# An attention and two-layer kernel: the gate's products are put in another order and alternate between two banks

## The chip, the cores and the metric

The kernel runs on one core of a Trainium2 chip. Its time is the device time of one execution in microseconds (us), taken over several executions. Five engines work beside each other, each through its own instructions in order: TensorE (PE; its weight loads are shown as PEld), VectorE (DVE), ScalarE (ACT), GpSimd (POOL) and SyncE (SP, which issues the DMAs). They wait for each other by semaphores. TensorE writes its results into PSUM, which has 8 banks of 512 float32 values in each of 128 partitions; VectorE and ScalarE read them from there.

## The reference

```
def _moe_ref(x, w1, w2, w3, w_out):
    a = x @ w1
    b = x @ w2
    h = a * b @ w3
    return (h @ w_out).astype(np.float32)

def _moe2_ref(x, w_in, w_out, g_ln):
    h = x @ w_in
    # solu = h * softmax(h), then a layer norm over the row with the gain g_ln
    ...
    return (ln @ w_out).astype(np.float32)

def reference(...):
    attn_out = _attn_ref(...)        # banded attention: a window of 128 keys and 4 sink keys
    x = ...                          # 4 batches of 768 tokens, 512 columns
    x = _moe_ref(x=x, ...)           # 512 -> 1024 -> 1024 -> 512
    return _moe2_ref(x=x, ...)       # 512 -> 1024 -> 512
```

The stage of this case is the gate: `a = x @ w1`, `b = x @ w2` and their product element by element, for 3072 tokens, 512 columns in and 1024 out.

## The kernel before, in words

The kernel has four parts behind each other: attention (which also multiplies `w3` and `moe_w_out` together), the gate, the hidden layer, and the second network with its norm. Each engine's instructions behind the attention come from one list of tasks. A planner (`arrange`, line 49) puts them in order. It gives each task a duration and a due time (its rank) and lets each engine take the task with the lowest rank among those that are ready by its own reckoning. In that reckoning a bank is free once its readers are done, bank by bank. The waits themselves are set when the program is built, and go by the tile that an instruction touches.

Every large matrix product is done in 7 products of half matrices instead of 8 (line 41, `FACTORS`). A factor is a half of the matrix or a sum of halves, and each is split into a high and a low part, so that three matmuls together give float32 accuracy. These splits are line 365 on VectorE (low part) and line 158 on ScalarE (high part); the sums are line 368.

In the gate a batch has four groups of columns, m = 0 to 3. A group has 14 products: k = 1 to 7 for both weights, z = 0 for `w1` and z = 1 for `w2`. In this text (k,z) is such a product. A product is 6 matmuls of 128x128 weights over 384 columns into one bank. Products go one on the other: on bank Y first 1, then 6, 7 and 4 are added to what is there; on bank Z first 5, then 3; on bank X stands 2 alone. What has to be kept from a state in between is copied out by ScalarE (line 158, `copy`) or added to something by VectorE (line 948, `two`) before the next product goes on top. So every product on Y but the first of a group waits for a reader of the product before it.

The 8 banks are four tiles of two banks each (line 888). Tile 0 holds X and Y of z = 0 (X0, Y0), tile 1 holds Z0 and X1, tile 2 holds Y1 and Z1; tile 3 is unused in the gate before the change. The batches come in the order 2, 3, 0, 1 (line 988). Beside the products VectorE, ScalarE and GpSimd convert and split the gate's remaining weights (in the first batch), convert later weights (in the second and third) and split the next batch's tokens.

`both` (line 984) is the order in which products are put on the list; it also sets (`when`) when each factor's parts are due. `product` (line 974) picks the bank, lines 1067 to 1096 the copies and additions of a group.

Of the kernel before, what the change touches and what calls it, by code (L numbers as in the profile page):

```python
# [123 lines left out]
def attention_moe_kernel(  # L124
# [27 lines left out]
    PE, DVE, ACT, POOL, SP = nc.tensor, nc.vector, nc.scalar, nc.gpsimd, nc.sync  # L152
# [9 lines left out]
    def ns_of(eng, n):  # L162

        return {"ACT": 188 + .834 * n, "DVE": 140 + 1.055 * n, "POOL": 159 + 2.2 * n}[eng]
# [12 lines left out]
    def path(stack, banded):  # L177
# [5 lines left out]
        xop = hold.rearrange("p (s u c n) -> p s u c n", s=7, u=2, c=2)  # L183

        xlie = {n: i for i, n in enumerate((1, 6, 5, 4, 0, 3, 2))}
# [224 lines left out]
        def pair_factors(side, pair, seven):  # L410

            four = pair.rearrange("p a (b n) -> p (a b) n", b=2)
            return factors(
                side, [four[:, i] for i in range(4)], lambda n: (seven[:, n, 0], seven[:, n, 1]), (four, seven)
            )
# [54 lines left out]
        def x_factors(b):  # L470
            x = x_t[b]
            blk = [x[:, 2 * k:2 * k + 2, S // 2 * n:S // 2 * (n + 1)] for n in range(2) for k in range(2)]
            return factors("right", blk, lambda n: (xop[:, xlie[n], 0], xop[:, xlie[n], 1]))
# [390 lines left out]
        else:  # L864
            general_fold()
            general_attention()
            for n in range(4):
                w, m = ("w1", "w2")[n % 2], n // 2
# [21 lines left out]
        bank = [t[:, i] for t in four_banks for i in range(2)]  # L890
# [34 lines left out]
        def op(eng, ns, rank, outs, ins, f, *args, after=0, both=False, then=None):  # L925

            r = set().union(*(toks(a) for a in ins)) if ins else set()
            w = set().union(*(toks(a) for a in outs))
            if then is not None:
                r.add(then)  # L930
            tasks.append((eng + "+" * (eng == "POOL" or both), ns, rank, "stage", f, args, r - w, w, after))

        def dma(rank, out, in_, then=None):

            size = 4
            for d in out.shape:
                size *= d
            op("SP", max(475, size / 320), rank, [out], [in_], lambda: SP.dma_start(out=out, in_=in_), after=2300, then=then)

        def copy(rank, out, in_, cols, eng="ACT"):  # L940
            if eng == "ACT":
                op("ACT", ns_of("ACT", cols), rank, [out], [in_], acopy, out, in_)
            else:
                op("DVE", ns_of("DVE", cols), rank, [out], [in_], lambda: DVE.tensor_copy(out=out, in_=in_))

        def two(eng, rank, out, a, b, cols, o=ALU.add):
            op(
                eng, ns_of(eng, cols), rank, [out], [a, b], lambda: engines[eng].tensor_tensor(out=out, in0=a, in1=b, op=o),  # L948
                both=eng == "DVE" and not {a.tensor.name, b.tensor.name} & banks,
            )  # L950
# [20 lines left out]
        X, Y, Z = 0, 1, 2  # L971
        BANK = {1: Y, 6: Y, 7: Y, 4: Y, 2: X, 5: Z, 3: Z}

        def product(k, z, rank, ns, width, left, right):

            b = bank[3 * z + BANK[k]][:, 0:width]
            (lh, ll), (rh, rl) = left, right
            items = []
            for c in range(len(lh)):
                items += [(lh[c], rh[c]), (lh[c], rl[c]), (ll[c], rh[c])]  # L980
            op("PE", ns, rank, [b], [*lh, *ll, *rh, *rl], run, b, items, k in (1, 2, 5))
            return b

        both = [(1, 0), (1, 1), (2, 0), (6, 0), (2, 1), (6, 1), (5, 0), (7, 0), (5, 1), (7, 1), (4, 0), (3, 0), (4, 1), (3, 1)]
        when = {}
        for i, (k, z) in enumerate(both):
            when.setdefault(k, i)
# [1 line left out]
        TH = S // 2  # L989
        now = 0.0  # L990
# [37 lines left out]
        for bi, b in enumerate(order):  # L1028
            if bi >= 2:
                dma(now - 40000, slots[b % 2], xd[b].rearrange("p c n -> p (c n)"))  # L1030
            if bi:
                parts_of(x_factors(b), 768, part_rank(1, now, MM), sums="DVE")
            for m in range(4):
                if bi == 0 and m > 1:
                    for u, w in enumerate(("w1", "w2")):
                        for i in range(2):
                            convert((w, m + 4 * i), pairs[np_ % 3][:, i], u, now - 18000 + 1000 * u)
                        parts_of(pair_factors("left", pairs[np_ % 3], group(w, groups[m])), 0, part_rank(0, now, MM))
                        np_ += 1
                if bi in (1, 2):  # L1040
                    for _ in range(2):
                        key = later.pop(0)
                        d = pairs[0][:, key[1] % 2]
                        rank = now + 20000
                        convert(key, d, 0, rank)
                        if key[0] == "wout":
                            sc = g_sb[:, key[1]:key[1] + 1]
                            op("ACT", 600, rank, [d], [g_sb], acopy, d, d, sc)
                        dma(rank, (win_d if key[0] == "win" else wout_d)[key[1]], d)
                if bi == 3 and m == 2:  # L1050
                    for k in range(4):
                        piece = wpiece[k % 3].rearrange("p (m h n) -> p m h n", m=2, h=2)
                        for h in range(2):
                            dma(now - 8000, piece[:, :, h, :], wf_d[k + 4 * h].rearrange("p (m n) -> p m n", m=2))
                        four = piece.rearrange("p m h n -> p (m h) n")
                        seven = wfop[k]
                        parts_of(
                            factors("left", [four[:, i] for i in range(4)], lambda n: (seven[:, n, 0], seven[:, n, 1]), (four, seven)),
                            0, lambda n, kind, k=k: now + 8000 + 2000 * k, sums="DVE",
                        )  # L1060
                gw = [group(w, groups[m]).rearrange("p s u (c n) -> p s u c n", c=2) for w in ("w1", "w2")]
                p_, u2, u3, cc = tmp[0:2], tmp[2:4], tmp[4:6], tmp[6]

                def send(i, t, rank):
                    dma(rank, ab_d[b][i][m], t)

                for k, z in both:
                    l, r = FACTORS[k]
                    bk = product(
                        k, z, now, MM, TH, [[gw[z][:, l, u, c, :] for c in range(2)] for u in range(2)],  # L1070
                        [[xop[:, xlie[r], u, c, :] for c in range(2)] for u in range(2)],
                    )
                    now += MM
                    if k in (1, 6, 7):
                        copy(now, {1: p_, 6: u2, 7: u3}[k][z], bk, TH)
                    if k == 2:
                        two("DVE", now + 2000, p_[z], bk, p_[z], TH)
                        if z:
                            two("DVE", now + 5000, p_[0], p_[0], p_[1], TH, ALU.mult)
                            send(0, p_[0], now + 5000)  # L1080
                    if k == 7:
                        two("DVE", now, u3[z], bank[3 * z + Z][:, 0:TH], u3[z], TH)
                        if z:
                            two("DVE", now + 5000, u3[0], u3[0], u3[1], TH, ALU.mult)
                            send(3, u3[0], now + 5000)
                    if k == 4:
                        if z:
                            two("DVE", now + 1000, cc, cc, bk, TH, ALU.mult)
                            send(1, cc, now + 5000)
                        else:  # L1090
                            copy(now + 1000, cc, bk, TH)
                    if k == 3:
                        two("DVE", now + 1000, u2[z], bk, u2[z], TH)
                        if z:
                            two("DVE", now + 5000, u2[0], u2[0], u2[1], TH, ALU.mult)
                            send(2, u2[0], now + 5000)
# [48 lines left out]
        for g in range(7 * B):  # L1145
            bi, i = divmod(g, 7)
            b, k = order[bi], seq[i]
# [10 lines left out]
            for z in range(2):  # L1158
                p_, u2, u3, cc = tmp[4 * z:4 * z + 4]
                bk = product(  # L1160
                    k, z, now, MM, TH, [[wfop[c][:, l, u, z * P:(z + 1) * P] for c in range(4)] for u in range(2)],
                    [[t[:, u, c] for c in range(4)] for u in range(2)],
                )
# [101 lines left out]
        for c in range(2 * PAIRS):  # L1265
# [6 lines left out]
            if c in (7, 11, 15, 19):  # L1272
                k = (c - 7) // 4
# [145 lines left out]
```

## Time and profile before

| | us |
|---|---|
| median of 3 runs | 927.65 (926.5 to 927.68) |
| the profiled execution | 927.59 |
| its span in the profile | 925.2 |
| TensorE busy | 888.6 (96%) |
| VectorE busy | 700.0 (76%) |
| ScalarE busy | 548.8 (59%) |
| GpSimd busy | 183.4 (20%) |
| the gate's first matmul, the hidden layer's last | 263.4, 638.1 |

All places in the trace are in us from the start of the span. A row of a stretch shows its bounds and length, then the busy us (and number of instructions) of PE, PEld, DVE, ACT and POOL, the granted clock of TensorE as a share of full speed, the busy share of the DMA engines, and GB/s. A row in order of time shows start, length, engine, line, operation, output and inputs with shape, how many instructions are drawn together, and in brackets how long the engine stood idle before, and what ended that. A row of waits shows who waited for whom, the us in total, how often, and the longest. Buffer numbers are left out there, so that all banks are called bank.

### The profile page before, as it was taken

To read this page: it belongs to the slowest core of one execution; us is meant where nothing else is said; L and a number is where in the kernel's file an instruction comes from. 1 tells how busy PE (TensorE), PEld (TensorE's weight loads), DVE (VectorE), ACT (ScalarE), POOL (GpSimd) and SP (SyncE) were. 2 spreads that over 40 slices of the span, in tenths; PEclk is the share of its full clock that TensorE was granted. 3 is DMA by queue.
4 is the path that set the end of the run, shared out by engine and by line. 5 is a ranking of instruction groups with operands and counts; after the bars stand their busy time and mean duration, and the time that the engine had idled before them with its cause. 6 is when DMAs were issued, how large, how long until landed. Compare 5 with 4: busy or idle time off the path is not lost.

```text
span 925.2 us, 15584 instructions
## 1 busy us (share of the span) xinstructions
PE 888.6 (96%) x5392; PEld 749.8 (81%) x5392; DVE 700.0 (76%) x1646; ACT 548.8 (59%) x1251; POOL 183.4 (20%) x243
## 2 busy tenths in 40 slices
PE   7999999999999899999998999999999999999996
PEld 3555665665579898989888999999888888999996
DVE  6988888676958786773776897794788877898761
ACT  6887877765746444752543566563667576755441
POOL 2664655451225322120000000000010011000000
PEclk9999999999999999999999999999999999999999
DMA  7566657632236367563132265443243343454411
GB/s 273 182 232 235 204 188 252 215 123 80 69 100 184 128 203 240 191 214 125 56 130 76 85 208 188 158 146 124 104 146 127 125 160 137 172 194 143 177 58 61
DMA packets 84760, 143.72 MB, mean 155 GB/s; under 512 B 6976, under 2 KB 58432, under 8 KB 82240
## 3 DMA queue, kind: packets, MB, share of 16 engines
q1 hardware_dynamic: 84672, 142.64, 46.1%
q8 instruction: 44, 0.72, 0.3%
q14 instruction: 44, 0.36, 0.1%
HBM read 95.43 MB, written 47.19 MB: 154 GB/s over the span
## 4 chain that ended last, share of the span: by engine, by line
PE 82%; DVE 12%; DMA 2%; issue 2%; ACT 1%; POOL 1%; SPq 0%; DVEq 0%; ACTq 0%; POOLq 0%
PE bank L155 56%; PE s L155 11%; PE pa L155 6%; PE pat L644 4%; DVE arF L948 3%; PE bank L1233 2%; DVE hold L365 2%; DVE g L365 2%; PE pn L656 1%; PE pn L650 1%; DVE ar L368 1%; DVE sa L600 1%; DMA arF<-in_moe_w_in_dram 1%; DVE ring L661 1%; DMA qk<-in_qk_dram 1%
## 5 line engine op out<-in xcount | busy, mean ns | idle before, releaser
L155 PE MATMUL bank<-hold,g 128*128 128x384 f32 x2016 | 360.7, 338 | 15.4 <-DVE arF L948 11.1
L155 PEld LDWEIGHTS bank<-hold,g 128*128 128x128 f32 x2016 | 349.8, 189 | 26.4 <-DVE arF L948 19.2
L155 PE MATMUL bank<-g,hold 128*128 128x512 f32 (+1 forms) x1080 | 202.2, 342 | 0.6 <-ACT ar L158 0.5
L155 PEld LDWEIGHTS bank<-g,hold 128*128 128x128 f32 x1080 | 169.2, 190 | 22.3 <-ACT ar L158 1.0
L158 ACT ACTIVATE arF<-bank 128x384 f32<-128x384 f32 (+1 forms) x160 | 80.8, 519 | 115.5 <-PE bank L155 80.5
L615 ACT ACTIVATE sa<-sa,st 128x288 f32<-128x288 f32 (+1 forms) x192 | 95.7, 501 | 20.3 <-DVE st L600 17.4
L600 DVE CUSTOM_DVE_ANT_0 sa<-s,masks 128x288 f32<-128x288 f32 (+1 forms) x192 | 76.8, 418 | 23.9 <-PE s L155 23.6
L948 DVE TENSOR_TENSOR arF<-bank,arF 128x384 f32<-128x384 f32 x96 | 53.0, 554 | 51.7 <-PE bank L155 23.4
L365 DVE TENSOR_TENSOR hold<-ar,hold 128x384 fp32r<-128x384 f32 (+2 forms) x137 | 84.6, 648 | 8.5 <-ACT hold L158 8.2
L1221 POOL TENSOR_TENSOR stt<-stt,half 128x1 f32<-128x1 f32 x24 | 17.3, 721 | 371.0 <-DVE stt L1219 363.2
L158 ACT ACTIVATE hold<-ar 128x384 fp32r<-128x384 f32 (+2 forms) x137 | 75.4, 586 | 18.0 <-DVE ar L368 13.8
L155 PE MATMUL s<-qk 64*128 64x288 f32 (+2 forms) x384 | 75.0, 439 | 8.0 <-DMA qk<-in_qk_dram 6.0
L158 ACT ACTIVATE ar<-bank 128x256 f32<-128x256 f32 (+1 forms) x80 | 33.8, 423 | 73.9 <-PE bank L155 73.5
L155 PE MATMUL bank<-g,g 128*128 128x256 f32 x504 | 66.3, 285 | 3.9 <-DVE ar L948 2.2
L661 DVE COPY ring<-pat 128x512 f32<-128x512 f32 (+1 forms) x96 | 60.9, 640 | 11.3 <-PE pat L644 10.9
L155 PEld LDWEIGHTS bank<-g,g 128*128 128x128 f32 x504 | 62.5, 192 | 5.5 <-DVE ar L948 3.0
L155 PEld LDWEIGHTS s<-qk 64*128 64x128 f32 x384 | 34.0, 193 | 35.9 <-issue 15.0
L155 PE MATMUL s<-hold 128*128 128x512 f32 x192 | 59.5, 423 | 0.0
L155 PE MATMUL pa<-ring,vn 128*64 128x256 f32 (+1 forms) x448 | 56.1, 357 | 1.5 <-DVE ring L661 1.0
L644 PE MATMUL pat<-identr,sa 128*128 128x128 f32 x352 | 56.5, 281 | 0.0
L948 DVE TENSOR_TENSOR ar<-bank,ar 128x256 f32<-128x256 f32 (+1 forms) x60 | 28.4, 475 | 32.9 <-ACT ar L158 19.1
L368 DVE TENSOR_TENSOR ar<-ar 128x256 f32<-128x256 f32 (+3 forms) x92 | 51.5, 571 | 0.8
(97 smaller groups left out, 1150.4 us busy)
## 6 DMA issues: line engine op xcount, KB each, us to landing
qk<-in_qk_dram SPq DMA_DIRECT2D x15, 1088.0 KB, 5.1
raw<-in_moe_w_dram SPq DMA_DIRECT2D x24, 512.0 KB, 5.1
abd<-arF SPq DMA_DIRECT2D x64, 192.0 KB, 2.0
lnd<-arF SPq DMA_DIRECT2D x48, 256.0 KB, 2.2
ar<-lnd SPq DMA_DIRECT2D x8, 1024.0 KB, 5.6
vn<-in_v_dram SPq DMA_DIRECT2D x16, 384.0 KB, 3.2
arF<-abd SPq DMA_DIRECT2D x8, 768.0 KB, 5.0
ar<-abd SPq DMA_DIRECT2D x8, 768.0 KB, 4.7
```

The lines of the kernel that those rows point to most:

```text
L155: PE.matmul(o, lhsT=l, rhs=r, start=start, stop=stop, skip_group_check=True)
L158: ACT.activation(out=o, in_=i, func=AF.Copy, scale=s)
L365: eng.tensor_tensor(out=lo, in0=src, in1=fl(hi), op=ALU.subtract)
L368: eng.tensor_tensor(out=out, in0=a, in1=b, op=ALU.add if sign > 0 else ALU.subtract)
L600: DVE.tensor_tensor_reduce(out=sa[s][:, h, :n], in0=s_bank[s_at(s, h)][:, :n], in1=m_qb[j, h], op0=ALU.add, op1=ALU.min, scale=-scale, sca ...
L615: ACT.activation(out=a[:, h, :n], in_=a[:, h, :n], func=AF.Exp, scale=-1.0, bias=st_t[s][:, h:h + 1], accum_out=rs_t[p, j // 2][:, i:i + 1],)
L644: PE.transpose(pt[:, h, u, :], a[:, h, o:o + P], ident)
L650: PE.transpose(pn[0:n + 2 * SINKS, s % 2, :], a[:, 256 - n:256 + 2 * SINKS], ident)
L661: DVE.tensor_copy(out=ring[:, :, 2 * j + u0:2 * j + 2, :], in_=pat_t.pop(s)[:, :, u0:, :])
L948: eng, ns_of(eng, cols), rank, [out], [a, b], lambda: engines[eng].tensor_tensor(out=out, in0=a, in1=b, op=o),
L1221: op("POOL", 550, rank + 900, [st[7]], [st[6]], lambda: POOL.tensor_tensor(out=st[7], in0=st[6], in1=half, op=ALU.pow))
L1233: PE.transpose(bk[:, i * P:(i + 1) * P], e[:, (4 * g + i) * P:(4 * g + i + 1) * P], ident)
```

## The change

Four things change, all in the gate. The order of the products of a group becomes 1, 2, 6, 5, 7, 3, 4, each for z = 0 and then z = 1. In groups with odd m, what went to bank Y goes to bank 6 + z, the two banks of tile 3. What is kept of product 5 is copied out by ScalarE behind 5, and the addition behind 7 reads Y and not Z; before, 7 was copied and Z was read. And the order of the factors' due times follows, since `when` is made from `both`.

```
-        def product(k, z, rank, ns, width, left, right):
+        def product(k, z, rank, ns, width, left, right, other=False):
-            b = bank[3 * z + BANK[k]][:, 0:width]
+            b = bank[6 + z if other and BANK[k] == Y else 3 * z + BANK[k]][:, 0:width]
...
-        both = [(1, 0), (1, 1), (2, 0), (6, 0), (2, 1), (6, 1), (5, 0), (7, 0), (5, 1), (7, 1), (4, 0), (3, 0), (4, 1), (3, 1)]
+        both = [(k, z) for k in (1, 2, 6, 5, 7, 3, 4) for z in range(2)]
...
-                        [[xop[:, xlie[r], u, c, :] for c in range(2)] for u in range(2)],
+                        [[xop[:, xlie[r], u, c, :] for c in range(2)] for u in range(2)], m % 2 == 1,
...
-                    if k in (1, 6, 7):
-                        copy(now, {1: p_, 6: u2, 7: u3}[k][z], bk, TH)
+                    if k in (1, 6, 5):
+                        copy(now, {1: p_, 6: u2, 5: u3}[k][z], bk, TH)
...
-                        two("DVE", now, u3[z], bank[3 * z + Z][:, 0:TH], u3[z], TH)
+                        two("DVE", now, u3[z], bk, u3[z], TH)
```

On TensorE, an inner group of the last batch stands in the program before like this, from (1,1) to (5,0). bank0, bank1, bank2 and bank3 are the four tiles; x5 or x6 are the matmuls of a product, x11 five of one and six of the next.

```order
L155 MATMUL bank2_3011<-hold_74,g23_3003 128x384 [waits DVE_49]
L155 MATMUL bank2_3011<-hold_74,g23_3003 128x384 x5
L155 MATMUL bank0_3009<-hold_74,g23_3003 128x384 [waits Activation_49]
L155 MATMUL bank0_3009<-hold_74,g23_3003 128x384 x11
L155 MATMUL bank1_3010<-hold_74,g23_3003 128x384 x6
L155 MATMUL bank2_3011<-hold_74,g23_3003 128x384 [waits Activation_49]
L155 MATMUL bank2_3011<-hold_74,g23_3003 128x384 x5
L155 MATMUL bank1_3010<-hold_74,g23_3003 128x384 [waits DVE_49]
L155 MATMUL bank1_3010<-hold_74,g23_3003 128x384 x5
```

The products are (1,1), (2,0) with (6,0), (2,1), (6,1) and (5,0). The first and the last wait for VectorE; (2,1) and (5,0) are both on bank1, with (6,1) between.

An odd group of the last batch now, from (1,0) and (1,1) to (5,1):

```order
L155 MATMUL bank3_3012<-hold_74,g01_73 128x384 x12
L155 MATMUL bank0_3009<-hold_74,g01_73 128x384 [waits Activation_49]
L155 MATMUL bank0_3009<-hold_74,g01_73 128x384 x5
L155 MATMUL bank1_3010<-hold_74,g01_73 128x384 x6
L155 MATMUL bank3_3012<-hold_74,g01_73 128x384 [waits Activation_49]
L155 MATMUL bank3_3012<-hold_74,g01_73 128x384 x11
L155 MATMUL bank1_3010<-hold_74,g01_73 128x384 [waits DVE_49]
L155 MATMUL bank1_3010<-hold_74,g01_73 128x384 x5
L155 MATMUL bank2_3011<-hold_74,g01_73 128x384 x6
```

The wait of (1,1) is gone, and between (2,1) and (5,0) on bank1 stand both 6 on bank3.

The second half of an even group of the last batch now, from (7,0) to (4,1):

```order
L155 MATMUL bank0_3009<-hold_74,g23_3003 128x384 x6
L155 MATMUL bank2_3011<-hold_74,g23_3003 128x384 [waits Activation_49]
L155 MATMUL bank2_3011<-hold_74,g23_3003 128x384 x5
L155 MATMUL bank1_3010<-hold_74,g23_3003 128x384 x6
L155 MATMUL bank2_3011<-hold_74,g23_3003 128x384 [waits DVE_49]
L155 MATMUL bank2_3011<-hold_74,g23_3003 128x384 x5
L155 MATMUL bank0_3009<-hold_74,g23_3003 128x384 x6
L155 MATMUL bank2_3011<-hold_74,g23_3003 128x384 [waits DVE_49]
L155 MATMUL bank2_3011<-hold_74,g23_3003 128x384 x5
```

(7,1), (3,1) and (4,1) are all on bank2 (Y1, Z1, Y1), with one product between each two, and each waits for a reader of the one before.

On VectorE, the rows before between the additions of X0 and of X1 in an even group of the last batch (line 365 are splits):

```order
L948 TENSOR_TENSOR arF_3004<-bank0_3009,arF_3004 128x384 [waits PE_49,Activation_49]
L365 TENSOR_TENSOR g23_3003<-arF_3004,g23_3003 128x512 [waits DMAHW5_49,Activation_49]
L365 TENSOR_TENSOR g01_73<-ar1_75,g01_73 128x2x256 [waits Activation_49] x2
L948 TENSOR_TENSOR arF_3004<-bank1_3010,arF_3004 128x384 [waits PE_49]
L948 TENSOR_TENSOR arF_3004<-arF_3004 128x384 [waits DVE_49]
```

The same place of the same group now, with the split that stands ahead of the first addition:

```order
L365 TENSOR_TENSOR g01_73<-ar1_75,g01_73 128x2x256 [waits Activation_49]
L948 TENSOR_TENSOR arF_3004<-bank0_3009,arF_3004 128x384 [waits PE_49]
L365 TENSOR_TENSOR g01_73<-ar1_75,g01_73 128x2x256 [waits Activation_49]
L948 TENSOR_TENSOR arF_3004<-bank1_3010,arF_3004 128x384 [waits PE_49]
L365 TENSOR_TENSOR g01_73<-ar1_75,g01_73 128x2x256 [waits Activation_49]
L948 TENSOR_TENSOR arF_3004<-arF_3004 128x384 [waits DVE_49]
```

One split stands between the two additions where three stood.

## Rows read from the trace of the kernel before

**Rows 1.** The page's first part, TensorE: busy us, share of the span, instructions.

```profile
PE 888.6 (96%) x5392; PEld 749.8 (81%) x5392; DVE 700.0 (76%) x1646; ACT 548.8 (59%) x1251; POOL 183.4 (20%) x243
```

**Rows 2.** Stretches: the gate's four batches in order, then the hidden layer.

```profile
263.40:329.60 66.20, 62.69 (x337) 59.63 (x338) 51.11 (x85) 35.91 (x70) 25.56 (x25) 0.97 0.48 150
329.60:393.20 63.60, 60.65 (x337) 57.81 (x336) 45.79 (x85) 37.26 (x75) 15.06 (x12) 1.00 0.67 224
393.20:456.20 63.00, 60.02 (x338) 58.10 (x337) 36.73 (x70) 26.23 (x54) 5.36 (x4) 1.00 0.40 134
456.20:521.70 65.50, 60.42 (x338) 57.95 (x338) 47.19 (x96) 29.61 (x61) 0.00 (x0) 1.00 0.32 101
521.70:640.00 118.30, 118.30 (x680) 117.75 (x679) 97.98 (x200) 66.71 (x141) 0.00 (x0) 1.00 0.52 166
```

**Rows 3.** Who waited for whom in the gate, TensorE's matmuls.

```profile
PE bank L155 <- DVE arF L948: 11.1, 16, 1.2
PE bank L155 <- ACT arF L158: 2.6, 4, 0.9
```

**Rows 4.** Order of time, TensorE, the last batch.

```profile
455.68 1.73 PE L155 MATMUL bank<-hold,g 128*128 128x384 f32 x9
458.02 5.50 PE L155 MATMUL bank<-hold,g 128*128 128x384 f32 x30 [0.61 <-DVE arF L948]
464.02 9.63 PE L155 MATMUL bank<-hold,g 128*128 128x384 f32 x54 [0.51 <-DVE arF L948]
474.40 5.48 PE L155 MATMUL bank<-hold,g 128*128 128x384 f32 x30 [0.74 <-DVE arF L948]
480.78 9.64 PE L155 MATMUL bank<-hold,g 128*128 128x384 f32 x54 [0.91 <-DVE arF L948]
491.16 5.48 PE L155 MATMUL bank<-hold,g 128*128 128x384 f32 x30 [0.74 <-DVE arF L948]
497.55 9.66 PE L155 MATMUL bank<-hold,g 128*128 128x384 f32 x54 [0.91 <-DVE arF L948]
507.88 14.30 PE L155 MATMUL bank<-hold,g 128*128 128x384 f32 x80 [0.67 <-DVE arF L948]
```

**Rows 5.** Order of time, TensorE, the third batch.

```profile
392.71 1.73 PE L155 MATMUL bank<-hold,g 128*128 128x384 f32 x9
395.04 5.49 PE L155 MATMUL bank<-hold,g 128*128 128x384 f32 x30 [0.61 <-DVE arF L948]
401.50 45.27 PE L155 MATMUL bank<-hold,g 128*128 128x384 f32 x252 [0.97 <-DVE arF L948]
447.75 8.44 PE L155 MATMUL bank<-hold,g 128*128 128x384 f32 x47 [0.98 <-DVE arF L948]
```

**Rows 6.** Order of time, VectorE, ahead of TensorE's pause at 497.55.

```profile
495.14 0.68 DVE L365 TENSOR_TENSOR g<-arF,g 128x512 fp32r<-128x512 f32 x1
495.74 1.29 DVE L365 TENSOR_TENSOR g<-ar,g 128x512 fp32r<-128x512 f32 x2
496.94 0.55 DVE L948 TENSOR_TENSOR arF<-bank,arF 128x384 f32<-128x384 f32 x1
```

**Rows 7.** Order of time, VectorE, a quiet group of the third batch.

```profile
425.19 0.56 DVE L948 TENSOR_TENSOR arF<-arF,bank 128x384 f32<-128x384 f32 x1 [1.59 <-PE bank L155]
425.66 0.55 DVE L948 TENSOR_TENSOR arF<-bank,arF 128x384 f32<-128x384 f32 x1
426.25 0.56 DVE L948 TENSOR_TENSOR arF<-arF 128x384 f32<-128x384 f32 x1
...
430.83 0.56 DVE L948 TENSOR_TENSOR arF<-bank,arF 128x384 f32<-128x384 f32 x1 [0.48 <-PE bank L155]
```

**Rows 8.** Order of time, TensorE, two pauses of the first batch.

```profile
302.93 11.87 PE L155 MATMUL bank<-hold,g 128*128 128x384 f32 x66 [0.92 <-ACT arF L158]
...
322.04 2.89 PE L155 MATMUL bank<-hold,g 128*128 128x384 f32 x12 [0.58 <-ACT arF L158]
```

**Rows 9.** Order of time, VectorE, an addition of two SBUF operands in the first batch.

```profile
271.84 1.51 DVE L948 TENSOR_TENSOR arF<-arF 128x384 f32<-128x384 f32 x1
```

## The prediction, made before the change was run

> **What bounds the kernel now.** I read the page's first part, then a table of stretches, then the waits, then the order of time on single engines.
>
> The page gives TensorE 96% of the span [rows 1]. A change that only moves waits can therefore win little, and only where TensorE pauses. The stretches show where that is [rows 2]. After the gate, the hidden layer runs 680 matmuls in 118.30 us with TensorE busy all the time: 0.174 us from one start to the next. The gate runs from 263.4 to 521.7, which is 258.3 us for 224 products of 6 matmuls, 1344 in all. At 0.174 these need 233.9, so 24.4 us are lost there. By batch of 336 matmuls (58.5 us) the loss is 7.7, 5.1, 4.5 and 7.0 us in the order of the four rows.
>
> The waits of that stretch say who ends the pauses [rows 3]: mostly VectorE's line 948 (the additions that read a bank), then ScalarE's line 158 (the copies).
>
> In the order of time on TensorE the counts name the product that pauses [rows 4, 5]. In the last batch stretches of 30 and 54 matmuls alternate, 5 and 9 products. Five products are (1,1), (2,0), (6,0), (2,1), (6,1); nine run from (5,0) to the next group's (1,0), where (k,z) is product k of weight z. So TensorE stops at two places per group: ahead of (1,1), which I call pause A, and ahead of (5,0), pause B. Each is sized by start + count x 0.174 against the next start. For the last batch: 0.77, 0.78, 0.98, 1.16, 0.98, 1.17 and 0.93, together 6.8 of the 7.0 lost. For the third batch: 0.76, 1.24, and 2.40 over the 252 matmuls to 447.75, together 4.4 of 4.5.
>
> Pause B is not a wait for the bank of (5,0) itself. That bank, Z0, shares a tile with X1, and the program's wait falls on the addition that reads X1, the result of (2,1), one product earlier. In the row order that addition stands behind three splits. The trace has them from 495.14, one of 0.68 and two in 1.29; the addition starts at 496.94, and TensorE resumes at 497.55, 0.06 after it ends [rows 4, 6]. In the quiet third batch the same wait costs nothing: 401.50 to 447.75 is one row, and VectorE stood idle 0.48 us before the addition at 430.83 [rows 5, 7]. Pause A is two additions behind each other (425.19 and 425.66) that are both held until (3,1) has ended, since Y1 and Z1 share a tile. It costs about 0.4 even with an idle VectorE: 2.40 less one pause B of 1.2 leaves 1.2 for three of them [rows 5, 7].
>
> **The change part by part.** No instruction is added or removed: matmuls, copies and additions keep their number and size. The copy of 7 becomes a copy of 5, and the addition that read Z reads Y. That costs nothing, since both are the same form.
>
> *Odd groups (m = 1, 3).* Y lies in the fourth tile, with nothing else in it. All waits there reach back two products or more. (1,1) has no wait of its own, and (5,0) waits for X1 with two products between instead of one, that is 1.04 us more. Pauses A and B go.
>
> *Even groups (m = 0, 2).* (1,1) now waits for (3,1) of the odd group before, with three products between, and (5,0) for X1 with two. Pauses A and B go here as well. But 3 ahead of 4 and 2,2,6,6 put new close waits on shared tiles, with one product between: (6,0) on the addition of X0, (3,1) on that of Y1, (4,1) on that of Z1. Counting them in the row order over all eight even groups gives 20, 11 of them in the last two batches. The trace of before bounds such a wait at 0 (the quiet B) and 1.17 (B behind three splits). One addition fits with about 0.07 us to spare (pause A's 0.4 less the 0.47 between its two additions). For (3,1) and (4,1) the additions of 7 and 3 stand one behind the other with at most a split between, so I take the value near the quiet row, 0.1; for (6,0) one split of 0.68 [rows 6] can stand ahead, so I take 0.5. In the last two batches that is 8 x 0.1 + 3 x 0.5 = 2.3.
>
> ScalarE gets more waits with one product between too, (5,1) and (7,1) on copies. Before, (2,0) has this wait on the copy of (1,0) in most groups, and none of the rows of the last two batches stops there [rows 4, 5]. I take 0; behind one split of ScalarE it could be 0.4 each.
>
> *Last two batches:* 11.2 of pauses go, 2.3 come: 8.9 gained.
>
> *First two batches:* 12.8 are lost. The granted clock of 0.97 over 66.2 us is 2.0 of that and stays [rows 2]; it is 1.00 elsewhere in the gate. The remaining 10.8 are mixed. Of TensorE's 11.1 us of idle behind VectorE's additions [rows 3], the pauses listed for the last two batches hold 7.65 (0.61, 0.97, 0.98; 0.61, 0.51, 0.74, 0.91, 0.74, 0.91, 0.67); 3.45 is left for the first two. Scaled by pause per idle (11.2 / 7.65) that is about 5 us of pauses of kinds A and B. ScalarE's 2.6 of idle lies here, with pauses like those at 302.93 and 322.04 [rows 8]; about 3.8 us by the same scale. Products of two groups are shuffled there because the weights' factors come late, and afterwards they still are. I let the 5 go, 1.5 of ScalarE's go, and charge the 9 other close waits 0.3 each (more splits stand about there): 5 + 1.5 - 2.7 = 3.8. Bounds: 0 to 9.
>
> In this stretch VectorE is slower as well: an addition of two SBUF operands took 1.51 us at 271.84 and 0.56 at 426.25 [rows 7, 9], and POOL is busy 25.56 us in the first batch and not at all in the last [rows 2]. *GPSIMD Engine Reference* of the Trainium skill, section 1 Specifications, says that GpSimd's SBUF interfaces are shared with VectorE and contend with its instructions that have two SBUF inputs; the trace agrees (1.51 against 0.56). By that rule a close wait in the first batch stays dear in any order, and without that batch's part (about 1.5) the time would be 916.4.
>
> *What cover there is.* Nothing behind the gate absorbs the gain: the hidden layer's TensorE row is full, and the order behind the gate is that of before. Its VectorE is busy 97.98 of 118.30 [rows 2], so there is room to follow an earlier start. In the gate VectorE's 47.19 us would stand in about 60 in the last batch, 79%.
>
> *Sum:* 8.9 + 3.8 = 12.7. The profiled execution took 927.59 us (span 925.2 and 2.4 around it): 927.6 - 12.7 = 914.9. The median of the runs is 927.65, so the same.
>
> **The rivals.**
> 1. *The close waits cost what B costs now.* B cost 0.78, 1.16, 1.17, 1.24 and about 1.2 in five of the last eight groups and nothing in three: 0.69 on average. 20 x 0.69 = 13.8 against 11.2 + 6.5 = 17.7: 3.9 gained, 923.7. This is also the case in which the change doesn't do what it says: three products lie between any two on a bank, yet in even groups only one between two on a tile. For it: VectorE is busy 77% of the first batch and 72% of the second and the last [rows 2]. Against it: the splits stand in the first half of a group, the new waits mostly in the second.
> 2. *All goes but the clock.* If no close wait were felt, 24.4 - 2.0 = 22.4 would go: 905.2. Against it: a split of 0.68 and only 0.07 to spare. The Trainium skill's page *PSUM — Partial Sum Buffer*, section *PSUM bank collisions raise a hardware error*, has software guard PSUM by bank and quadrant. By that rule alone there would be no close wait here, and this rival would be the forecast; the trace differs, since pause B ends with an addition on another bank.
> 3. *Slower: the pairs in the fourth tile.* In odd groups the products of a pair, say (1,0) and (1,1), write one tile, so the reader of the first is held until the second has ended, 1.04 us at the head of ScalarE's or VectorE's queue. Four pairs in eight groups are 33 us of held queues, with the splits for the next factors behind them. It decides from the point where more than 17.7 of the 33 reaches TensorE. At three quarters it is 25: 7 slower, 934.6. Against it: ScalarE is idle about half of the gate and the reuse of a pair's banks is two products off.
>
> **How the numbers follow.** Forecast 0.65 (its own range 909 to 920), rival 1 0.19, rival 2 0.11, rival 3 0.05. Low 905.0 takes in rival 2, high 923.5 half of rival 1. A difference of 0.2%, 1.9 us, is what a measurement of this kernel can tell. Faster: forecast, rival 2 and most of rival 1, 0.92. Same: a part of rival 1, 0.03. Slower: rival 3, 0.05.
>
> **What the profile after would show.** On TensorE the alternating stretches of 30 and 54 are gone and odd groups run through. What pauses are left stand in even groups ahead of (6,0), (3,1) or (4,1), and in the first batch. The idle behind line 948 falls from 11.1 to about 4, the gate to about 246 us, and the hidden layer keeps 118.3. If pauses of near 1 us stand at (3,1) and (4,1), rival 1 holds. If odd groups stop as well, or ScalarE's copies hold TensorE, rival 3 does. If TensorE stops behind the gate, the cover was wrong.

## The result, and the profile after

The changed kernel takes 911.2 us (median of 4 runs, 909.7 to 912.79), the kernel before, in runs on the same chip, 927.08 (924.66 to 927.68). The ratio is 0.983, 95% interval 0.981 to 0.986. The forecast was 914.9, with a range of 905.0 to 923.5.

The profiled execution of the changed kernel took 910.68, with a span of 908.9. The page's first part, as [rows 1]:

```profile
PE 881.7 (97%) x5392; PEld 748.2 (82%) x5392; DVE 697.8 (77%) x1646; ACT 546.3 (60%) x1251; POOL 183.1 (20%) x243
```

All instruction counts are those of before. The span is 16.3 us shorter, TensorE's busy time only 6.9; the rest of it was idle time of TensorE. The four batches of the gate and the hidden layer, as [rows 2]:

```profile
262.08:324.56 62.48, 60.12 (x336) 58.14 (x337) 46.53 (x80) 35.26 (x71) 24.90 (x24) 1.00 0.48 154
324.56:385.38 60.82, 59.90 (x337) 58.08 (x337) 47.66 (x88) 34.98 (x68) 14.42 (x11) 1.00 0.67 221
385.38:445.18 59.80, 59.25 (x337) 58.20 (x337) 37.21 (x73) 27.81 (x56) 6.50 (x5) 1.00 0.48 160
445.18:504.96 59.78, 59.22 (x338) 58.20 (x337) 47.06 (x98) 28.99 (x62) 0.00 (x0) 1.00 0.34 111
504.96:623.26 118.30, 118.30 (x680) 117.75 (x680) 97.90 (x200) 66.71 (x142) 0.00 (x0) 1.00 0.51 166
```

The gate takes 242.9 us where it took 258.3. By batch the gain is 3.7, 2.8, 3.2 and 5.7 us, and 4.0, 2.4, 1.3 and 1.3 of loss against the pure 58.5 are left. The hidden layer has kept its 118.30. So 15.4 of the 16.3 us come from the gate; its start is 1.3 us earlier and the time behind it 0.4 longer. Who waited for whom in the gate, TensorE's matmuls, as [rows 3]:

```profile
PE bank L155 <- DVE arF L948: 3.2, 5, 1.2
...
PE bank L155 <- ACT arF L158: 0.9, 2, 0.5
```

The idle behind VectorE's additions fell from 11.1 us in 16 pauses to 3.2 in 5. In order of time on TensorE, from the gate's start to the hidden layer, as [rows 4, 5]:

```profile
262.08 32.16 PE L155 MATMUL bank<-hold,g 128*128 128x384 f32 x180 [0.91 <-DVE ar L703]
294.67 3.40 PE L155 MATMUL bank<-hold,g 128*128 128x384 f32 x18 [0.43 <-ACT arF L158]
299.26 9.88 PE L155 MATMUL bank<-hold,g 128*128 128x384 f32 x54 [1.19 <-DVE arF L948]
309.87 26.88 PE L155 MATMUL bank<-hold,g 128*128 128x384 f32 x150 [0.74 <-DVE arF L948]
337.01 30.03 PE L155 MATMUL bank<-hold,g 128*128 128x384 f32 x168 [0.26 <-DVE arF L948]
367.59 27.36 PE L155 MATMUL bank<-hold,g 128*128 128x384 f32 x156 [0.55 <-DVE arF L948]
395.43 54.09 PE L155 MATMUL bank<-hold,g 128*128 128x384 f32 x306 [0.47 <-ACT arF L158]
449.99 171.82 PE L155 MATMUL bank<-hold,g 128*128 128x384 f32 x984 [0.47 <-DVE arF L948]
```

The alternation of 30 and 54 matmuls is gone. In the last two batches only two pauses are long enough for a row of their own: at 395.43 ahead of (7,1) of the third batch's first group, and at 449.99 ahead of (6,0) of the last batch's first group, both even. VectorE ahead of the second:

```profile
447.51 0.56 DVE L948 TENSOR_TENSOR arF<-arF 128x384 f32<-128x384 f32 x1
447.98 1.49 DVE L365 TENSOR_TENSOR hold<-ar,hold 128x384 fp32r<-128x384 f32 x3
449.38 0.55 DVE L948 TENSOR_TENSOR arF<-bank,arF 128x384 f32<-128x384 f32 x1
```

This is the picture of [rows 6] again: three splits ahead of the addition, and TensorE resumes 0.06 us after it. The reader of X0, one product behind, now has the place that the reader of X1 had.

### The profile page after: what moved, and what is told of

The parts are those of the page before. It is cut to its first block, busy times and chain, and to the rows that moved or that the text cites. A ratio compares the mean times of both kernels' runs of the same rounds, so it can differ in the third digit from the quotient of the medians.

```text
span 908.9 us, 15588 instructions
## 1 busy us (share of the span) xinstructions
PE 881.7 (97%) x5392; PEld 748.2 (82%) x5392; DVE 697.8 (77%) x1646; ACT 546.3 (60%) x1251; POOL 183.1 (20%) x243
## 4 chain that ended last, share of the span: by engine, by line
PE 84%; DVE 10%; ACT 2%; DMA 2%; issue 1%; SPq 0%; POOL 0%; DVEq 0%; ACTq 0%
PE bank L155 62%; PE s L155 10%; PE pa L155 5%; PE pat L644 3%; PE bank L1233 2%; DVE hold L365 2%; DVE sa L600 1%; DVE arF L948 1%; PE pn L656 1%; DVE ring L661 1%; PE pn L650 1%; DVE ar L368 1%; DMA raw<-in_moe_w_dram 1%; DVE g L365 1%; DMA qk<-in_qk_dram 1%
## 5 line engine op out<-in xcount | busy, mean ns | idle before, releaser
L155 PE MATMUL bank<-hold,g 128*128 128x384 f32 x2016 | 355.3, 336 | 5.3 <-DVE arF L948 3.2
L158 ACT ACTIVATE hold<-arF 128x384 fp32r<-128x384 f32 (+2 forms) x82 | 41.9, 553 | 18.1 <-DVE arF L368 5.7
```

The lines of the kernel that those rows point to most:

```text
L155: PE.matmul(o, lhsT=l, rhs=r, start=start, stop=stop, skip_group_check=True)
L158: ACT.activation(out=o, in_=i, func=AF.Copy, scale=s)
```

## The experiments

All eight are compared with the kernel before on the same chip: 926.6 us in the first four, 926.56 in the last four. The theory was that the waits go by the tile of two banks: a reader (a copy or an addition) starts when the last product put on its tile before it has ended, and the next product on that tile waits for the reader. By the theory TensorE pauses where only one other product stands between these two products; such a wait is called a close wait. The rivals were that the gain comes from the alternation itself (the bank), and that VectorE's queue holds the product in any arrangement.

**Order alone.** The new order and copies, Y always in its own bank.

```
-                        ... for u in range(2)], m % 2 == 1,
+                        ... for u in range(2)], False,
...
```

> The new order of products alone; bank Y is not alternated. Theory (tile): a pause is a wait for a reader of the same two-bank tile with one product between, priced by what stands ahead of that reader. By the row order the waits of that kind on VectorE are 26 here (23 before the change, 20 after), those on ScalarE 44 (18, 24). Pauses A and B go by the order, the close waits of even groups then stand in all groups: about 915 (913 to 919), gate about 247 us. Rival (bank): what counts is that two products on one bank have three others between, so without the second bank pause A returns in all groups and the time is 920 to 924.

Measured: 911.15 us (910.45 to 912.45), ratio 0.984 [0.982, 0.985]. TensorE in order of time, from late in the second batch to the gate's end:

```profile
364.67 44.10 PE L155 MATMUL bank<-hold,g 128*128 128x384 f32 x246 [1.19 <-ACT arF L158]
410.06 3.40 PE L155 MATMUL bank<-hold,g 128*128 128x384 f32 x18 [1.30 <-DVE arF L948]
413.63 94.61 PE L155 MATMUL bank<-hold,g 128*128 128x384 f32 x538 [0.17 <-ACT arF L158]
```

The 538 matmuls from 413.63 to 508 need 93.6 at 0.174 and took 94.6. As a whole program, the new order without alternation brings all that the change brings (911.15 against 911.2; the profiled gates take 244.0 and 242.9). Both the theory's number (my size of a close wait) and the bank rival were too high. Counted in the row order, this kernel has 26 close waits for VectorE, the changed kernel 20 and the kernel before 23, so their number alone is not what costs.

This is not the changed kernel with one thing taken away. Without the second bank the planner puts (2,0) ahead of (1,0) in nearly every group, so two products and not one stand between (6,0) and the last one before it on its tile, and no pause stands ahead of (6,0) in the last two batches. What the alternation adds when the order stays the same is not shown. Nor are two products between always enough: the pause of 1.30 at 410.06 stands ahead of (5,0), and the reader that it waits for came late because VectorE had waited 2.59 us for a DMA.

**Alternation alone.** The order of before in the list, Y alternating between its own tile and tile 3.

```
-            b = bank[3 * z + BANK[k]][:, 0:width]
+            b = bank[6 + z if other and BANK[k] == Y else 3 * z + BANK[k]][:, 0:width]
...
-                        ... for u in range(2)],
+                        ... for u in range(2)], m % 2 == 1,
```

> The alternation of bank Y alone, with the old order and the old copy of 7. Theory (tile): pause A goes, since (1,1) of every second group lies on tile 3 or has its readers on a tile that it does not touch; pause B stays, since (5,0) still stands one product behind (2,1) on its tile (15 such waits by the row order, 11 before): 918 to 921, and the order of time on TensorE shows pauses ahead of (5,0). Rival (queue): the pauses went because the splits moved in VectorE's order, so the banks alone bring nothing: 926 to 928.

Measured: 921.44 us (920.77 to 922.49), ratio 0.996 [0.994, 0.997], just above the theory's 918 to 921. TensorE, last batch:

```profile
449.62 8.59 PE L155 MATMUL bank<-hold,g 128*128 128x384 f32 x48 [0.74 <-ACT arF L158]
458.71 15.07 PE L155 MATMUL bank<-hold,g 128*128 128x384 f32 x84 [0.51 <-DVE arF L948]
474.31 9.85 PE L155 MATMUL bank<-hold,g 128*128 128x384 f32 x54 [0.53 <-DVE arF L948]
484.41 5.50 PE L155 MATMUL bank<-hold,g 128*128 128x384 f32 x30 [0.24 <-DVE arF L948]
490.81 16.35 PE L155 MATMUL bank<-hold,g 128*128 128x384 f32 x90 [0.91 <-DVE arF L948]
507.67 8.66 PE L155 MATMUL bank<-hold,g 128*128 128x384 f32 x47 [0.51 <-ACT arF L158]
```

Pause B is left: VectorE stops TensorE ahead of (5,0) at 458.71, 474.31 and 490.81 (Z0 and X1 share a tile as before). Of pause A one is left in this batch, ahead of (1,1) at 484.41. New pauses come behind ScalarE. Who waited for whom in this gate:

```profile
PE bank L155 <- ACT arF L158: 5.5, 8, 1.1
PE bank L155 <- DVE arF L948: 4.3, 9, 0.9
```

ScalarE's part was 2.6 us before [rows 3]. With the alternation both Y of an odd group share tile 3, and in the old order only one product stands between (6,0), (7,0) or (4,1) and the product before on that tile, which ScalarE has to copy; the row at 449.62 begins with such a (4,1), the one at 507.67 with such a (7,0). So the alternation alone brought 5.2 us of the median and paid part of its gain back.

**Placement alone.** The order of before, instruction by instruction; in the gate X1 moves to bank 6 and Z1 to bank 7, so that no close neighbours share a tile. No alternation.

```
-            b = bank[3 * z + BANK[k]][:, 0:width]
+            b = bank[{X: 6, Y: 4, Z: 7}[BANK[k]] if gate and z else 3 * z + BANK[k]][:, 0:width]
...
-                        two("DVE", now, u3[z], bank[3 * z + Z][:, 0:TH], u3[z], TH)
+                        two("DVE", now, u3[z], bank[7 if z else Z][:, 0:TH], u3[z], TH)
```

> The kernel before, its order of products one for one, no alternation; only X1 and Z1 move in the gate to the two banks of tile 3, so that Z0 and Y1 have their tiles to themselves. Theory (tile): (5,0) no longer waits for the reader of X1, and the readers of Y1 and Z1 are no longer held by each other, so pauses A and B go without any change of order: 912 (910 to 916). Rival (bank) and rival (queue): distances on a bank and VectorE's order are those of before: 926 to 928.

Measured: 910.37 us (908.83 to 912.83), ratio 0.984 [0.982, 0.986]; the theory said 912 (910 to 916). TensorE, from the second half of the second batch to the gate's end:

```profile
364.33 38.77 PE L155 MATMUL bank<-hold,g 128*128 128x384 f32 x222 [0.82 <-ACT arF L158]
403.56 101.69 PE L155 MATMUL bank<-hold,g 128*128 128x384 f32 x585 [0.45 <-ACT arF L158]
```

In the last two batches both pauses are gone in the order that had them: 585 matmuls run through, at 0.174 each, with VectorE's instructions in the same order as before. This settles that pauses A and B were waits for another bank of the same tile; the bank rival and the queue rival both wanted 926 to 928 here.

**One bank of the two.** The order of before, only X1 moved to bank 6 (Z1 stays with Y1).

```
-            b = bank[3 * z + BANK[k]][:, 0:width]
+            b = bank[{X: 6, Y: 4, Z: 5}[BANK[k]] if gate and z else 3 * z + BANK[k]][:, 0:width]
...
```

> The kernel before with its order of products, and only X of z = 1 moved to bank 6 in the gate (Z1 stays beside Y1 in tile 2). This separates pause B from pause A. Theory (waits go by the tile of two banks): pause B, ahead of (5,0), goes in all groups, pause A, ahead of (1,1), stays. B is 8 x 0.69 = 5.5 us of the last two batches and about 2.5 of the first two, so 926.6 - 8 = 918.6 (916.5 to 921), and in the trace the last two batches still show a pause per group, 0.4 to 0.8 us each, ahead of (1,1). Rival (the bank itself or VectorE's queue holds the product): no change, 925 to 928, with pauses at both places. If the two pauses hang together (a pause removed only gives VectorE less time at the next), under 4 us are gained, 922.5 or more.

Measured: 919.26 us (917.78 to 921.2), ratio 0.992 [0.990, 0.995]: the theory's 918.6. TensorE, last batch:

```profile
453.80 14.86 PE L155 MATMUL bank<-hold,g 128*128 128x384 f32 x84 [0.61 <-DVE arF L948]
469.40 14.84 PE L155 MATMUL bank<-hold,g 128*128 128x384 f32 x84 [0.74 <-DVE arF L948]
484.98 14.84 PE L155 MATMUL bank<-hold,g 128*128 128x384 f32 x84 [0.74 <-DVE arF L948]
500.49 14.75 PE L155 MATMUL bank<-hold,g 128*128 128x384 f32 x83 [0.67 <-DVE arF L948]
```

Where 30 and 54 alternated [rows 4], each row now holds one group of 84: one pause per group, ahead of (1,1). Taking B away is worth 7.3 us of the medians, and moving Z1 as well, which takes A away, another 8.9 (7.7 between the two profiled gates, 249.6 and 241.9).

**Pairs by kind.** The changed kernel, with X0 and X1 in one tile, Y0 and Y1 in the next, Z0 and Z1 in the third. Every engine's order is that of the changed kernel; the close waits fall from 20 to 2 on VectorE and from 24 to 6 on ScalarE. It was timed twice, the second time beside the changed kernel.

```
-            b = bank[6 + z if other and BANK[k] == Y else 3 * z + BANK[k]][:, 0:width]
+            b = bank[3 * z + BANK[k] if other is None else 6 + z if other and BANK[k] == Y else 2 * BANK[k] + z][:, 0:width]
...
```

> The changed kernel with one difference: in the gate a tile holds the two banks of one kind (X0 X1, Y0 Y1, Z0 Z1), so both products of a pair share a tile and the next product on that tile is two products off. The order of the products is that of the changed kernel, one for one. Theory (tile): close waits fall from 44 to 8, the pauses left in even groups of batches 2 to 4 go, and the gate loses about 5 us instead of 10: 906 (904 to 908.5). Rival (bank): the same banks are as far from each other as in the changed kernel, so nothing changes: 911. Rival (pairs): the reader of the first of a pair is held until the second ends, now in all groups, so it is slower than the changed kernel: 914 or more.

> The alternating pairs by kind once more (X0 with X1, Y0 with Y1, Z0 with Z1 in one tile on even groups, Y in tile 3 on odd groups, new order): 906.8 (905.5 to 908.5), 4.4 below the changed kernel. If the earlier gap was a matter of the chip or the run, it comes within 1.5 us of the changed kernel.

> The changed kernel once more, in more rounds and on the same chip as the two versions with pairs by kind: 911.2 (909.7 to 912.8), ratio to before 0.983 to 0.985. It tells whether the 4 us between it and the pairs by kind hold in one comparison.

Measured: 906.84 us (905.93 to 908.58), ratio 0.979 [0.978, 0.981]; again 906.37 (904.74 to 907.48), ratio 0.978 [0.975, 0.981]. The changed kernel beside the second took 913.76 (912.15 to 916.11), ratio 0.987 [0.984, 0.990], a little above its forecast of 909.7 to 912.8. So the pairs beat both kernels, the changed one by 4 to 7 us (the two gates profiled in the second comparison differ by 4.2). The four batches and TensorE's rows of the second run:

```profile
263.68:323.25 59.57, 59.05 (x337) 58.30 (x337) 47.74 (x80) 34.84 (x71) 24.74 (x24) 1.00 0.50 162
323.25:383.81 60.56, 59.36 (x338) 58.14 (x337) 46.45 (x88) 34.34 (x68) 14.44 (x11) 1.00 0.69 221
383.81:442.94 59.13, 59.05 (x337) 58.18 (x337) 37.16 (x74) 27.05 (x56) 6.51 (x5) 1.00 0.49 163
442.94:501.43 58.49, 58.49 (x338) 58.23 (x337) 47.10 (x98) 28.26 (x62) 0.00 (x0) 1.00 0.35 113
```

```profile
263.68 23.50 PE L155 MATMUL bank<-hold,g 128*128 128x384 f32 x132 [0.91 <-DVE ar L703]
287.65 58.89 PE L155 MATMUL bank<-hold,g 128*128 128x384 f32 x336 [0.48 <-ACT arF L158]
347.44 19.00 PE L155 MATMUL bank<-hold,g 128*128 128x384 f32 x108 [0.90 <-ACT arF L158]
366.68 134.57 PE L155 MATMUL bank<-hold,g 128*128 128x384 f32 x766 [0.24 <-DVE arF L948]
```

The last batch takes 58.49, the pure matmul time. Only three pauses are long enough to end a row behind the gate's first.

**Pairs by kind without alternation.** The same tiles, Y always in its own. As in the order alone, the planner then puts (2,0) ahead of (1,0).

```
-                        ... for u in range(2)], m % 2 == 1,
+                        ... for u in range(2)], False,
...
```

> The pairs by kind (X0 with X1, Y0 with Y1, Z0 with Z1 in one tile, in the new order) without the alternation: Y stays in its own tile in all four groups. Theory A, that the alternation matters once no other bank shares a tile: product 4 of a group and product 1 of the next go on the same tile one behind the other, which makes a wait with one product between ahead of (1,0) in every group, and 15 + 22 such waits in all where the alternating version has 2 + 6. At 0.3 us for the 15 on VectorE and 0.1 for the 22 on ScalarE that is 6.7 us over the alternating pairs: 913.5 (910.5 to 916). Theory B, that a wait with one product between costs nothing in the new order, as the order alone without alternation showed: as the alternating pairs, 906.8 (905.5 to 908.5).

Measured: 921.8 us (919.15 to 924.32), ratio 0.995 [0.993, 0.997]. Theory A had the direction and half the size: 15.4 us over the alternating pairs, where 6.7 were expected. In the gate 15.3 of it shows (253.05 against 237.75). TensorE, last batch:

```profile
457.42 15.24 PE L155 MATMUL bank<-hold,g 128*128 128x384 f32 x84 [0.44 <-ACT arF L158]
473.10 15.29 PE L155 MATMUL bank<-hold,g 128*128 128x384 f32 x84 [0.44 <-ACT arF L158]
488.83 27.43 PE L155 MATMUL bank<-hold,g 128*128 128x384 f32 x151 [0.43 <-ACT arF L158]
```

A row of 84 without a pause lasts 14.84 (one bank of the two) and here 15.24: a pause of 0.41 ahead of (1,0) hides in it (the starts inside the row show it), and the pause that begins each row is that of (6,0). (1,0) follows (4,1) with one product, (2,0), between. Since Y0 and Y1 share a tile, both readers of 4 are held until (4,1) has ended, and they run one behind the other: ScalarE's copy of (4,0), then VectorE's multiplication (line 948 too) of that copy with (4,1). VectorE ahead of the (1,0) that starts at 469.27:

```profile
468.66 0.56 DVE L948 TENSOR_TENSOR arF<-arF,bank 128x384 f32<-128x384 f32 x1 [0.99 <-ACT arF L158]
```

That is pause A again, two readers behind one product, with its price: (1,0) paused 0.41 to 0.43 in seven of the last eight groups, and 1.06 in the other. (6,0) does the same with the two copies of 1 on ScalarE, 0.20 to 0.75 in seven of the eight. So leaving the alternation out cost nothing where banks of different products share a tile (order alone), and 15 us where a pair does; in both the planner's order moved with it.

## Why the prediction was right, step by step

**What bounds the kernel.** Right, and shown by the placement alone: the last two batches lost their time at A and B, and moving two banks without touching the order removes both. The cover behind the gate was read correctly too: the hidden layer's row is 118.30 in both.

**Last two batches, 8.9 gained.** Measured 8.9 (128.5 less 119.6). The sum came out to the tenth partly by luck, since inside it the terms moved. Starts show 2.5 us of pauses where 2.3 of close waits were charged, but in other places: (6,0) took 0.75 and 0.37 in two groups (1.5 in three was charged), (3,1) and (4,1) nothing at all (0.8 was charged), and (7,1), (7,0) and (4,0) took 0.77, 0.32 and 0.32. ScalarE's close waits were taken at 0, with 0.4 each possible behind one split; (7,1) at 395.43 is the one that was not free. Its copy stood on ScalarE behind another instruction, a conversion of later weights:

```profile
394.34 0.66 ACT L158 ACTIVATE arF<-arF 128x512 f32<-128x512 f32 x1
394.89 0.49 ACT L158 ACTIVATE arF<-bank 128x384 f32<-128x384 f32 x1
```

A copy that holds TensorE was to be a sign of rival 3; this one stands in an even group, in which tile 3 is not used. Odd groups do not quite run through: the two 0.32 stand in two of them, and in the pairs by kind at the same two products.

**First two batches, 3.8 gained.** Mis-sized: 6.5 (129.8 less 123.3). The term that failed is the 2.0 of TensorE's clock that was said to stay. The profiled execution of before ran at half clock when the gate began, that of after did not. The gate's first 4 us, before and then after:

```profile
263.38:267.38 4.00, 4.00 (x14) 4.00 (x15) 0.00 (x0) 0.53 (x2) 0.00 (x0) 0.57 0.72 230
```

```profile
262.08:266.08 4.00, 4.00 (x23) 4.00 (x24) 0.51 (x2) 1.22 (x3) 0.00 (x0) 1.00 0.72 226
```

Nine matmuls fewer, 1.6 us at 0.174; the 2.0 had come from the rounded 0.97. TensorE had stood idle 0.91 us ahead of its first gate matmul in both, so the trace does not say why only one fell. Without the clock, 4.9 of pauses went where 3.8 were forecast. The prediction had placed only 8.8 (5 and 3.8) of the 10.8 that it counted as pauses there.

**The sum.** 927.6 less 12.7 gave 914.9. Between the two profiled spans the gate gave 15.4 and its earlier start 1.3, less 0.4 behind it: 16.3. The 3.6 beyond the 12.7 are 1.6 of clock in the gate, 1.1 of pauses in the first two batches and 0.9 outside the gate.

The medians, 15.9 apart, hold some clock as well. The executions of before in the later comparisons show it: nine with a mean granted clock of 0.999 of full speed took 923.31 to 925.19 us, thirteen at 0.995 took 926.33 to 928.23. The forecast started from 927.65, with a profiled execution at 0.993; three of the four executions behind 911.2 ran at 0.998 or 0.999. At like clock the change is worth 13.5 us (0.998 and 0.999: medians 924.17 and 910.68) or 14.1 (0.995: 926.76 and 912.62). So the forecast of 12.7 was about 1 us short, and some 2 of the 3.7 us between 914.9 and 911.2 come from the executions that were compared, not from the change.

**Rival 1 (close waits at the price of B).** Refuted by the changed kernel itself (20 close waits at 0.69 would cost 13.8 us, and its gate lost 9.0 in all) and by the order alone: at 0.69 each its 26 would cost 18 us, and its gate lost 10.1 in all (244.0 less 233.9). The working that did hold is the one for pause A: one addition fits beneath one product with 0.07 us to spare, two leave about 0.4. A close wait with one reader is nearly free unless other work stands ahead of that reader; one with two readers behind each other cost 0.4 or more in each of the last eight groups of the version without alternation.

**Rival 2 (all goes but the clock, 905.2).** Its mechanism fell: with banks instead of tiles as the guard, the placement alone could not have moved the time, and it moved it by 16.2 us. Its number is nearly reached by the pairs by kind, at 906.4, which leave 2 close waits for VectorE. *PSUM — Partial Sum Buffer* of the Trainium skill, section *PSUM bank collisions raise a hardware error*, asks software to guard PSUM by bank and quadrant. This program's waits guard by the tile, which is more than that rule asks for, and the placement shows what that cost here: 16.2 us.

**Rival 3 (pairs in the fourth tile make it slower).** Refuted as it stood: in the pairs by kind all pairs share a tile and the kernel is faster still. Its mechanism exists, though. The pairs by kind without alternation show it, where the tile's next product comes with one product between instead of two or more, and so does the alternation alone with most of its 5.5 us behind ScalarE.

**The first batch.** *GPSIMD Engine Reference* of the Trainium skill, section 1 Specifications, says that GpSimd's SBUF interfaces are shared with VectorE and contend with its instructions that have two SBUF inputs. The prediction made of it a possible first batch without any gain, 916.4. The changed kernel gained 3.7 in that batch, 1.6 of it clock. VectorE's contention with GpSimd does not keep the batch dear in any order: the pairs by kind lose 1.1 us in it (59.57 less 58.5) with GpSimd busy 24.74 us, where the changed kernel loses 4.0 with 24.90. What a close wait costs beside a busy GpSimd these rows do not show, since the pairs leave almost none there.

## What to carry to other kernels

Where a program's waits go by allocation, the unit that matters is the tile and not the bank: lay the banks of one tile out so that the next product on any of them stands at least two products behind the last one that is read. Price a close wait by what has to pass on the reader's queue after the product has ended: one addition, which holds VectorE for 0.47 us, hides beneath a product of 1.04; two readers behind each other, or one addition behind three splits, do not. Order, placement and alternation all act on that distance; before the second is added, try each alone. Here the order or the placement sufficed by itself, and the alternation alone brought 5 of 16 us. And look at the order that comes out: leaving the alternation out of the new order also changed what the planner put first.

## What the hardware showed that was not expected

TensorE's clock had stretches at half speed (the lower of its two levels, 1.2 instead of 2.4 GHz) in the attention, which the change doesn't touch, in some profiled executions and not in others. From 24 to 36 us the mean granted clock was 0.86 before, 1.00 after, 0.72 with the order alone and 1.00 with the placement alone. With it the gate's start moved: 263.38, 262.08, 263.34 and 261.60. Differences of 1 to 3 us between two profiled spans can come from there, so a change in the gate is better read from the gate's own length.

The changed kernel itself came out at 911.2 and at 913.76 in two comparisons, 0.3% apart, with the kernel before at 927.08 and 926.56. Its two profiled gates took 242.9 and 242.0, so the difference lies outside the gate. The granted clock goes with it: three of the first four executions ran at 0.998 or 0.999 and took 909.7 to 911.73, the fourth at 0.995 took 912.79; the later six ran at 0.992 to 0.995 and took 912.15 to 916.11. Why it falls in some executions and not in others no run here shows.
